# Agent attention with a squared-ReLU layer on one core: another order of the first blocks, and shared places for attention's matmuls

## Chip, cores and metric

One core of one Trainium2 chip. The metric is the device time of one execution in microseconds (us), median of the runs.

## What is computed

For each of B = 4 batches, `q`, `k` and `v` are 12480 x 128, with 49 agents; `w_in` is 128 x 2048, `w_out` 2048 x 128.

```
a2k     = softmax(agents @ k.T / sqrt(128))        # 49 x 12480
agent_v = a2k @ v                                  # 49 x 128
q2a     = softmax(q @ agents.T / sqrt(128))        # 12480 x 49
x       = q2a @ agent_v
y       = relu(x @ w_in) ** 2 @ w_out
```

## The kernel before

The queries are cut into 52 groups of 960 (13 of a batch). For a group and each of the 16 slices of 128 hidden columns there is one **block** i, from 0 to 831. Matmuls keep fp32 accuracy by splitting an operand into a rounded high part and the rest. `agent_v @ w_in` is made once a batch (`w_make`, parts `w_a` and `w_b`), so the first layer of a block (`mm1`, line 423) takes the 49 probabilities of each query (`p_a`, `p_b`) straight to the hidden slice: three pairs of matmuls. Two matmuls of a pair run on the two halves of TensorE's rows at once. ScalarE applies ReLU (`relu`, line 427) and squares (`square`, line 433) into `g`. `high` copies `g` to the rounded `gh`: by a DMA that GpSimd issues (line 438) for all blocks below 48 and for even ones after that, by VectorE else. `low` (VectorE, line 444) makes `gl = g - gh`. The second layer (`mm2`, line 462) is six pairs a block, from `gh` with `wo_hi` and `wo_lo` and from `gl` with `wo_hi`, added up over a group in one of two pairs of PSUM banks (`out`); from block 24 on two blocks are taken together. The first layer writes into two other pairs of banks (`h`, `new_h()`), by turns. Between two matmuls of `mm2` that change the bank of a row half stands a relay: an empty GpSimd instruction that waits for the first and frees the second.

Attention runs between the blocks. `q_scores` (line 169) makes the scores of two groups of queries, then six steps on VectorE and ScalarE turn them into probabilities (`q_turn`, `q_max`, `q_sub`, `q_exp`, `q_total`, `q_norm`, `q_back`), and eight DMAs of SyncE spread them (`q_spread`). For the next batch, keys come in seven parts (`k_scores`, then `k_copy` by ScalarE and `k_max` by VectorE), then `k_exp`, `k_turn`, and values in seven parts (`v_acc`, 28 matmuls on TensorE, then `v_sum` by VectorE). These matmuls use TensorE's rows as one, not as two halves. Before, `q_scores` and `v_acc` write into the pair of `out` banks that the current group doesn't use (`att()`, `bank()`), `k_scores` into `h`.

The order of everything is a list of (time, function), where time 1 is one block: `at(t, f, ...)`. Each engine works through its part of the sorted list in that order. The head up to block 24 is written by hand (lines 597 to 693 and 707 to 725); after that `chain()` looks for the first free time for a step, with `taken` and `banks` as the tables of what is in use. `SKIP` names blocks at which the second layer pauses. I call a **place** a point between two blocks at which attention's matmuls are inserted; `plan_queries`, `plan_keys` and `plan_values` choose them. In the head, `win_make` and `wo_make` convert the weights from 64-bit floats, four parts each, mostly on VectorE (`to_f32`, lines 85 to 90), and `wo_split` makes `wo_hi` by a DMA of GpSimd and `wo_lo` by a subtraction on GpSimd (two parts) or VectorE.

Of the kernel before, what the change touches and what calls it, by code (L numbers as in the profile page):

```python
# [13 lines left out]
AF = mybir.ActivationFunctionType  # L14
ALU = mybir.AluOpType
# [12 lines left out]
def agent_attention_relu2_kernel(ctx: ExitStack, tc: tile.TileContext, qT, kT, v, agT, w_in, w_out, outT):  # L28
# [6 lines left out]
    nc = tc.nc  # L35
# [5 lines left out]
    NSG = qT.shape[1] // ST  # L41
# [90 lines left out]
    kts, vts, pes, pss = {}, {}, {}, {}  # L132
# [4 lines left out]
    def new_h():  # L137
        return ps_h.tile([P, 2, 512], F32, name="h")
# [10 lines left out]
    def bank():  # L149
        return att()[:, 0]  # L150
# [74 lines left out]
    def v_acc(n, xs=(0, 1), ps=None):  # L225
        first, last = (n, n) if ps is None else (0, NP - 1)
        if ps is None:
            ps = pss["v", n] = bank()
        for x in xs:
            vt = vts.pop(2 * n + x)  # L230
            for y in range(VC):
                c = x * VC + y
                t = 64 * (c % 2)
                nc.tensor.matmul(ps[t:t + A, :C + 1], pes[n][:, c, :A], vt[:, y, :], start=n == first and c < 2, stop=n == last and c >= KC - 2)  # L234
            if x:
                pes.pop(n)
# [166 lines left out]
    hs, gs, ghs, gls = {}, {}, {}, {}  # L403
# [23 lines left out]
        nc.scalar.activation(gs[i], hs.pop(i)[:, :, :TT], AF.Relu)  # L427

    def square(i):
        if i in (1, 3):  # L430
            nc.gpsimd.tensor_tensor(gs[i], gs[i], gs[i], op=ALU.mult)
        else:
            nc.scalar.activation(gs[i], gs[i], AF.Square)  # L433

    def high(i):
        ghs[i] = ew.tile([P, 2, TT], F32R, name="gh", bufs=HB)
# [48 lines left out]

    LAG = 8
    TAIL = 36
    SKIP = (6, 9, 12)

    def by_dma(i):  # L490
        return i < NG - 4 and (i % 2 == 0 or i < 3 * NF)
# [3 lines left out]
    def at(t, f, *args):  # L495
        steps.append((t, len(steps), f, args))
# [5 lines left out]
    taken = {(e, s * NF + NF - 1 + LAG) for s in range(NSG) for e in ("DVE",)}  # L502
    banks = {s * NF + NF - 1 + LAG + x for s in range(NSG) for x in range(3)}
# [34 lines left out]

    def plan_queries(u):

        first, t = chain(max(18, 32 * u - 60), [("PE", q_scores, u), ("DVE", q_turn, u)])
        for x, s in enumerate(members(u)):
            at(first - LEAD + .1 * x, q_load, s)
        plan_rows(u, t + 2, 32 * u - 37)

    def plan_rows(u, g, free):
        todo = [("DVE", q_max, u), ("DVE", q_sub, u), ("ACT", q_exp, u), ("DVE", q_total, u), ("DVE", q_norm, u), ("DVE", q_back, u)]
        for e, f, _ in todo:
            _, t = chain(g, [(e, f, u)])
# [7 lines left out]
            _, t = chain(max(t, s * NF - 9 if s > 1 else 0), [("POOL" if s > 1 else "ACT", q_hi, s), ("DVE", q_lo, s)])  # L557
            assert t + 1 < s * NF, (s, t)

    def plan_keys(b, n, t):  # L560

        while ("PE", t) in keyed:
            t += 1
        keyed.add(("PE", t))
# [8 lines left out]
    keyed = set()  # L573
# [5 lines left out]
    def plan_values(b, t0, stop):  # L579

        used, turned = {}, {}
        d = (stop - TAIL - t0) / NP
        for n in range(NP):
            _, t1 = turned[n] = chain(max(t0 + 1 + int(n * d), used.get(n - 2, 0)), [("ACT", k_exp, n), ("DVE", k_turn, n)])
            used[n], end = chain(t1 + 3, [("PE", v_acc, n), ("DVE", v_sum, n)])
            for x in range(2):
                at(used[n] - LEAD + .1 * x, v_load, b, 2 * n + x)
        last, end = chain(end + 2, [("PE", a_final, 0), ("DVE", a_final, 1), ("DVE", a_final, 2)])
        assert end < stop - 6, (b, end, stop)
        if b < B - 1:  # L590
            for n in range(NP):
                _, keys = plan_keys(b + 1, n, used[n])
            return max(last + 2, plan_bias(keys + 1))


# [14 lines left out]
    Z = -100.0  # L610
    order, t = {}, 6.4
# [18 lines left out]
    for n, (f, *args) in enumerate(loads):  # L630
        t = order["v", 3] if f is q_load and args[0] else 0
# [15 lines left out]
    t = order["b", 3]  # L647
# [11 lines left out]
    t = order["q", 0] + 1.75  # L659
# [3 lines left out]
    t = last  # L663
# [7 lines left out]
    for n in range(2):  # L671
        for x, y in ((0, 2), (2, 3), (3, 3.5)):
            at(Z + t + y + .1 * n if n == 0 or x == 0 else .05 + .01 * x, w_first, x, n)
    for f, t in ((1, 1), (2, 2)):
        for x, y in ((0, .02), (2, .15), (3, .2)):
            at(t + y + (.1 if f == 2 and x else 0), w_make, 0, f, x)
    convert(win_make, 3, [y - Z for y in (6.7, 6.71, 6.72, 7.2, 7.7, 8.5)])
    for n, t, y0, y1 in ((0, (.13, .14, .15, .6, .7, .8), 2.35, 4.1), (1, (1.3, 1.31, 1.32, 2.1, 2.4, 2.45), 4.2, 6.2),
                         (2, (9.1, 9.11, 9.3, 10.1, 10.3, 11.1), 11.9, 14.3), (3, (12.1, 12.12, 12.3, 13.1, 13.3, 14.1), 14.9, 17.3)):
        convert(wo_make, n, [y - Z for y in t])  # L680
        at(y0, wo_split, n, 0)
        at(y1, wo_split, n, 1)
    for t in (1.45, 2.45, 4.45):
        at(t, warm_up, 3, 0)
    at(3.06, warm_up, 2, 0)
    at(3.07, begin)
    at(3.08, q_scores, 1)
    banks.update(range(12))
    for f, t in ((q_turn, 4), (q_max, 4.1), (q_sub, 4.6), (q_exp, 5.5), (q_total, 6.1), (q_norm, 6.6), (q_back, 7.6), (q_spread, 8.1)):
        at(t, f, 1)  # L690
    plan_halves(1, 13)
    for x, y in enumerate((.005, .02, .5, 1.4)):
        at(9 + y, w_make, 0, 3, x)
    for b in range(1, B):
        for f, x in enumerate((-6, -3, 0, 4)):
            first, end = chain(b * NS * NF + x, [("PE", w_make, b, f, 0), ("PX", w_make, b, f, 1), ("ACT", w_make, b, f, 2), ("DVE", w_make, b, f, 3)])
            assert x >= 4 * f - 12 and end < b * NS * NF + min(4 * f, LAG), (b, f, first, end)
    for u in range(2, NSG // 2 + 1):
        plan_queries(u)
    t = 20  # L700
    for n in range(NP):
        t, end = plan_keys(1, n, t + 3)
    ready = plan_bias(end + 1)
    for b in range(1, B):
        ready = plan_values(b, ready, b * NS * NF)

    for i in range(NG):
# [65 lines left out]
```

## Time and profile before

| | |
|---|---|
| median of 3 runs (lowest, highest) | 1740.31 us (1739.79, 1746.88) |
| the profiled execution's own time | 1742.1 us |
| its span, first to last instruction | 1740.3 us |
| mean granted TensorE clock | 0.997 |
| busy: PE / PEld | 99% / 86% |
| busy: VectorE / ScalarE / GpSimd | 86% / 92% / 16% |

The span is what the profile's rows cover; the profiled execution took 1.8 us more than it. A timeline row gives the start, the length, the engine, the line in the kernel, what is written from what, and the count; a bracket gives idle time before the row and what ended it. PE rows overlap, since matmuls are pipelined: starts are to be compared, not ends.

### The profile page before, as it was taken

Reading aid. Unit: us, or ns where it says so; the run is one execution under the profiler, and the core shown is the slowest. Engines: PE = TensorE matmul, PEld = TensorE weight load, DVE = VectorE, ACT = ScalarE, POOL = GpSimd, SP = SyncE. Lnnn points to the kernel's source line nnn. Section 1 sums busy time; section 2 is a strip of 40 time slices with the busy share of each in tenths; the row PEclk is TensorE's granted clock in tenths of the full one; section 3 lists DMA queues with packets and bytes.
Section 4 is the critical chain, followed back from the end, with each engine's and each line's share of the span. In section 5 each row is a group of like instructions: output and inputs, shape, how many; then the busy total and the mean of one; then the engine's idle time right before and its main releaser. Section 6 shows DMA issues by size and latency. Waiting matters only on the chain.

```text
span 1740.3 us, 41683 instructions
## 1 busy us (share of the span) xinstructions
PE 1717.3 (99%) x16833; PEld 1501.7 (86%) x16833; DVE 1490.3 (86%) x1744; ACT 1593.3 (92%) x1802; POOL 271.6 (16%) x508
## 2 busy tenths in 40 slices
PE   8899999999999999999999999999999999999998
PEld 4577888888888888988988898898898899999998
DVE  6877898898888898898898898898888889889887
ACT  4688998999998999999999999999999999999997
POOL 0322111111111111111111111111111111111110
PEclk9999999999999999999999999999999999999999
DMA  9799667648556646646646555565653555555452
GB/s 371 268 314 333 218 204 235 219 148 256 178 179 208 224 145 227 222 144 225 198 160 211 174 187 190 176 194 184 195 192 134 194 186 173 173 189 179 153 174 105
DMA packets 113506, 349.72 MB, mean 201 GB/s; under 512 B 15566, under 2 KB 28128, under 8 KB 113312
## 3 DMA queue, kind: packets, MB, share of 16 engines
q0 software_dynamic: 70976, 227.46, 38.6%
q1 hardware_dynamic: 42336, 119.59, 21.2%
q8 instruction: 132, 2.16, 0.5%
q14 instruction: 62, 0.51, 0.1%
HBM read 81.47 MB, written 25.56 MB: 61 GB/s over the span
## 4 chain that ended last, share of the span: by engine, by line
PE 91%; DMA 3%; issue 2%; DVE 2%; ACT 2%; SPq 0%; POOL 0%; DVEq 0%; POOLq 0%; ACTq 0%
PE out L462 55%; PE h L423 27%; PE ps_att L169 3%; PE ps_att L234 2%; PE h L169 2%; DMA gh<-g 2%; ACT g L433 1%; DMA vt<-v 1%; DVE gl L444 1%; PE ps_att L317 1%; DMA kt<-kT 1%; PE out L605 0%; PE out L234 0%; DVE e L353 0%; ACT g L427 0%
## 5 line engine op out<-in xcount | busy, mean ns | idle before, releaser
L444 DVE TENSOR_TENSOR gl<-g,gh 128x960 fp32r<-128x960 f32 x832 | 935.0, 1148 | 45.4 <-DMA gh<-g 37.2
L427 ACT ACTIVATE g<-h 128x960 f32<-128x960 f32 x832 | 812.8, 977 | 89.0 <-PE h L423 88.9
L433 ACT ACTIVATE g<-g 128x960 f32<-128x960 f32 x830 | 834.7, 1006 | 0.0
L462 PE MATMUL out<-gh,wo_hi 64*128 64x480 f32 x3328 | 621.7, 369 | 4.0 <-POOLq L456 3.3
L462 PE MATMUL out<-gh,wo_lo 64*128 64x480 f32 x3328 | 609.7, 362 | 0.0
L462 PE MATMUL out<-gl,wo_hi 64*128 64x480 f32 x3328 | 478.6, 364 | 3.5 <-DVE gl L444 3.5
L438 POOL DMA_DIRECT2D gh<-g x438 | 232.8, 531 | 1419.2 <-ACT g L433 727.3
L462 PEld LDWEIGHTS out<-gh,wo_hi 64*128 64x128 f32 x3328 | 314.2, 184 | 67.1 <-issue 36.3
L440 DVE CAST gh<-g 128x960 fp32r<-128x960 f32 x394 | 258.1, 655 | 127.0 <-ACT g L433 126.5
L462 PEld LDWEIGHTS out<-gl,wo_hi 64*128 64x128 f32 x3328 | 316.1, 186 | 28.6 <-DVE gl L444 7.9
L462 PEld LDWEIGHTS out<-gh,wo_lo 64*128 64x128 f32 x3328 | 317.4, 186 | 21.3
L423 PE MATMUL h<-p_a,w_a 49*128 49x480 f32 x1664 | 310.4, 369 | 0.6 <-ACT w_a L301 0.5
L423 PE MATMUL h<-p_a,w_b 49*128 49x480 f32 x1664 | 305.3, 363 | 0.0
L423 PE MATMUL h<-p_b,w_a 49*128 49x480 f32 x1664 | 304.4, 361 | 0.0
L423 PEld LDWEIGHTS h<-p_a,w_a 49*128 49x128 f32 x1664 | 158.8, 187 | 14.1 <-ACT w_a L301 1.5
L423 PEld LDWEIGHTS h<-p_b,w_a 49*128 49x128 f32 x1664 | 160.2, 188 | 10.3
L423 PEld LDWEIGHTS h<-p_a,w_b 49*128 49x128 f32 x1664 | 156.8, 184 | 12.6 <-DVE w_b L303 0.4
L353 DVE STREAM_TRANSPOSE e<-ps_att 128x960 f32<-128x960 f32 (+1 forms) x26 | 30.7, 1182 | 36.1 <-PE ps_att L169 36.1
L478 DVE COPY ob<-out 128x960 f32<-128x960 f32 x51 | 58.7, 1150 | 2.0 <-PE out L462 1.7
L184 ACT COPY sk<-h 128x896 f32<-128x896 f32 x28 | 25.3, 904 | 29.9 <-PE h L169 26.0
L169 PE MATMUL h<-kt,ag_sb 128*32 128x448 f32 x448 | 49.3, 545 | 1.9 <-DVE mxs L187 1.0
L169 PE MATMUL ps_att<-qt,ag_sb 128*32 128x480 f32 x408 | 47.2, 572 | 1.0 <-DVE w_b L328 1.0
(96 smaller groups left out, 585.0 us busy)
## 6 DMA issues: line engine op xcount, KB each, us to landing
gh<-g POOLq DMA_DIRECT2D x438, 480.0 KB, 3.5
vt<-v SPq DMA_DIRECT2D x56, 451.5 KB, 6.9
kt<-kT SPq DMA_DIRECT2D x56, 448.0 KB, 7.7
qt<-qT SPq DMA_DIRECT2D x52, 480.0 KB, 4.7
outT<-ob SPq DMA_DIRECT2D x51, 480.0 KB, 3.0
pt<-et SPq DMA_DIRECT2D x204, 60.0 KB, 3.6
p_a<-pt POOLq DMA_DIRECT2D x50, 211.9 KB, 3.5
raw<-w_in SPq DMA_DIRECT2D x4, 512.0 KB, 10.7
```

Source lines behind the costliest of these rows:

```text
L169: nc.tensor.matmul(ps[32 * j:32 * j + 32, h, :w], ags[j // 2][:, 32 * h:32 * h + 32], xs[j // 2][:, j % 2 * w:j % 2 * w + w], start=True, ...
L184: nc.scalar.copy(sk[:, n], pss["k", n][:, :, :KW])
L234: nc.tensor.matmul(ps[t:t + A, :C + 1], pes[n][:, c, :A], vt[:, y, :], start=n == first and c < 2, stop=n == last and c >= KC - 2)
L353: nc.vector.transpose(squares(es[u]), pss.pop(("q", u))[r, :, :TT].rearrange("p h (b c) -> p h b c", c=32))
L423: nc.tensor.matmul(hs[i][:, t, :TT], w, two(p), start=n == 0, stop=n == 2)
L427: nc.scalar.activation(gs[i], hs.pop(i)[:, :, :TT], AF.Relu)
L433: nc.scalar.activation(gs[i], gs[i], AF.Square)
L438: nc.gpsimd.dma_start(out=ghs[i], in_=gs[i])
L440: nc.vector.tensor_copy(ghs[i], gs[i])
L444: nc.vector.tensor_tensor(out=gls[i], in0=gs.pop(i), in1=ghs[i].bitcast(F32), op=ALU.subtract)
L462: mm = nc.tensor.matmul(o[:, u, :TT], w[rows, j, :], two(g[rows, u, :]), start=first and n == 0, stop=last and n == len(todo) - 1)
L478: nc.vector.tensor_copy(ob, o[:, :, :TT])
```

## The change

Five things are done.

1. Blocks 1 and 3 are squared by ScalarE like all others; before, GpSimd did it (`square`).
2. In the head, `w_make` of slices 1 and 2 stands at 0.5 and 1.6 (was 1 and 2), `w_make` of slice 3 at 7 (was 9), the conversion of the last part of `w_in` at 2 to 3 (was 6.7 to 8.5), that of `w_out`'s first two parts behind it; the second layer starts at block 6 (was 5) and pauses at 7 and 12 (was 6, 9 and 12); `low` of the first blocks comes 0.5 to 0.9 later, and blocks 6 to 9 take the timing of the later ones (`high` at i + 3.05, was i + 1.3).
3. `v_acc` writes into the first layer's banks (`new_h()`), with no gap kept for them in `banks`.
4. The planners share places: `shared` records the places of keys and values, `plan_queries` takes one of them where it finds one from 66 to 50 blocks before 32u, and the seven parts of batch 1's keys stand at 18 (two, with queries), 24 (two), 29 and 33 (two), where they had seven places of their own from 23 to 41.
5. Queries are planned after keys and values, and start up to two blocks earlier.

```
-            ps = pss["v", n] = bank()
+            ps = pss["v", n] = new_h()[:, 0]
...
-        if i in (1, 3):
-            nc.gpsimd.tensor_tensor(gs[i], gs[i], gs[i], op=ALU.mult)
-        else:
-            nc.scalar.activation(gs[i], gs[i], AF.Square)
+        nc.scalar.activation(gs[i], gs[i], AF.Square)
...
-    SKIP = (6, 9, 12)
+    SKIP = (7, 12)
...
-        first, t = chain(max(18, 32 * u - 60), [("PE", q_scores, u), ("DVE", q_turn, u)])
+        near = [t for t in sorted(shared) if 32 * u - 66 <= t <= 32 * u - 50 and t > rowed[-1] and not banks & set(range(t, t + 3))]
+        first, t = chain(near[0] if near else max(18, 32 * u - 62), [("PE", q_scores, u), ("DVE", q_turn, u)])
...
-            used[n], end = chain(t1 + 3, [("PE", v_acc, n), ("DVE", v_sum, n)])
+            t = t1 + 3
+            while t in shared or banks & set(range(t, t + 3)):
+                t += 1
+            used[n], end, shared[t] = t, t + 2, (b, n)
+            taken.add(("DVE", t))
+            at(t + .51, v_acc, n)
+            at(t + .55, v_sum, n)
...
-    for f, t in ((1, 1), (2, 2)):
-        for x, y in ((0, .02), (2, .15), (3, .2)):
-            at(t + y + (.1 if f == 2 and x else 0), w_make, 0, f, x)
-    convert(win_make, 3, [y - Z for y in (6.7, 6.71, 6.72, 7.2, 7.7, 8.5)])
+    for f, t in ((1, .5), (2, 1.6)):
+        for x, y in ((0, .005), (2, .02), (3, .56)):
+            at(t + y, w_make, 0, f, x)
+    convert(win_make, 3, [y - Z for y in (2, 2.01, 2.02, 2.6, 3, 3.02)])
...
-        at(9 + y, w_make, 0, 3, x)
+        at(7 + y, w_make, 0, 3, x)
...
-        t, end = plan_keys(1, n, t + 3)
+        t, end = plan_keys(1, n, (18, 18, 24, 24, 29, 33, 33)[n], "first")
...
-        if i < 10:
-            at(i + (1.3 if i else .2), high, i)
-            at(i + 4.4, low, i)
+        if i < 6:
+            at(i + (1.3 if i else .4), high, i)
+            at(i + (5.3 if i else 4.9), low, i)
```

The order shows three places. First VectorE in the head, from the first `low` on (`gl`). Before:

```order
L444 TENSOR_TENSOR gl<-g,gh 128x960
L361 TENSOR_TENSOR e<-e,mx 128x15x49
L444 TENSOR_TENSOR gl<-g,gh 128x960
L369 TENSOR_REDUCE sm<-e 128x15
L370 TENSOR_SCALAR sm<-sm 128x15
L371 RECIPROCAL sm<-sm 128x15
L444 TENSOR_TENSOR gl<-g,gh 128x960
L375 TENSOR_TENSOR e<-e,sm 128x15x49
L85 TENSOR_SCALAR cv_p<-raw 128x512
L87 TENSOR_SCALAR cv_x<-raw 128x512
L88 SCALAR_TENSOR_TENSOR cv_x<-raw,cv_x 128x512
```

And in the change, from the same point:

```order
L441 TENSOR_TENSOR gl<-g,gh 128x960
L357 TENSOR_REDUCE mx<-e 128x15
L361 TENSOR_TENSOR e<-e,mx 128x15x49
L441 TENSOR_TENSOR gl<-g,gh 128x960 x2
L369 TENSOR_REDUCE sm<-e 128x15
L370 TENSOR_SCALAR sm<-sm 128x15
L371 RECIPROCAL sm<-sm 128x15
L375 TENSOR_TENSOR e<-e,sm 128x15x49
L441 TENSOR_TENSOR gl<-g,gh 128x960
L328 SCALAR_TENSOR_TENSOR w_b_696<-ps_att,rc,w_a_695 113x512
```

The conversion of `w_in`'s last part (`cv_p`, `cv_x` from `raw`) no longer stands between the first `low`s, `q_max` (`mx`, line 357) has moved behind the first `low`, and the `w_b` of slice 3 follows the fourth `low`.

Second, TensorE after the first layer of block 18 (a row counts instructions, of which a score or value matmul makes two in the trace). Before:

```order
L423 MATMUL h<-p_a,w_b_498 128x480 x2
L462 MATMUL out<-gh,wo_hi 128x480 x2
L462 MATMUL out<-gh,wo_lo 128x480 x2
L462 MATMUL out<-gl,wo_hi 128x480 x2
L169 MATMUL ps_att<-qt,ag_sb 32x480 x8
L462 MATMUL out<-gh,wo_hi 128x480 x2
```

And now:

```order
L423 MATMUL h<-p_a,w_b_498 128x480 x2
L459 MATMUL out<-gh,wo_hi 128x480 x2
L459 MATMUL out<-gh,wo_lo 128x480 x2
L459 MATMUL out<-gl,wo_hi 128x480 x2
L169 MATMUL ps_att<-qt,ag_sb 32x480 x8
L169 MATMUL h<-kt,ag_sb 32x448 x16
L459 MATMUL out<-gh,wo_hi 128x480 x2
L459 MATMUL out<-gh,wo_lo 128x480 x2
```

Two parts of keys follow the queries, where each had a place of its own.

Third, TensorE where values come after queries: before, block 100, with values and keys seven blocks later,

```order
L423 MATMUL h<-p_b,w_a_535 128x480 x2
L423 MATMUL h<-p_a,w_b_536 128x480 x2
L169 MATMUL ps_att<-qt,ag_sb 32x480 x8
L462 MATMUL out<-gh,wo_hi 128x480 x2
L462 MATMUL out<-gh,wo_lo 128x480 x2
```

and in the change block 106:

```order
L423 MATMUL h<-p_a,w_b_696 128x480 x2
L169 MATMUL ps_att<-qt,ag_sb 32x480 x8
L234 MATMUL h<-vt,pe 49x129 x14
L169 MATMUL h<-kt,ag_sb 32x448 x8
L459 MATMUL out<-gh,wo_hi 128x480 x2
L459 MATMUL out<-gh,wo_lo 128x480 x2
```

Queries, values and keys stand in a row, and the values go to `h`. From block 18 on there were 53 places for queries, keys and values (25 of queries, 7 of keys, 21 of values, 14 of these with keys); in the change there are 41.

## Rows read from the trace of the kernel before

**Rows 1.** Page, part 1: busy time, share of the span, instructions of each engine
```profile
PE 1717.3 (99%) x16833; PEld 1501.7 (86%) x16833; DVE 1490.3 (86%) x1744; ACT 1593.3 (92%) x1802; POOL 271.6 (16%) x508
```

**Rows 2.** Stretches: busy us (count) of PE, PEld, DVE, ACT, POOL; clock, DMA share, GB/s
```profile
75.00:100.00 25.00, 20.88 (x180) 16.57 (x180) 18.71 (x26) 20.66 (x24) 5.83 (x11) 0.93 0.85 272
125.00:150.00 25.00, 25.00 (x238) 17.45 (x236) 18.13 (x18) 20.08 (x23) 5.51 (x11) 1.00 1.13 344
200.00:300.00 100.00, 100.00 (x1008) 85.75 (x1006) 85.64 (x99) 90.76 (x105) 13.84 (x26) 1.00 0.67 225
```

**Rows 3.** Timeline of PE: start, us, line, out<-in, count; a place for queries
```profile
346.70 0.36 PE L423 MATMUL h<-p_a,w_b 49*128 49x480 f32 x2
347.00 1.82 PE L169 MATMUL ps_att<-qt,ag_sb 128*32 128x480 f32 x16
348.75 0.47 PE L462 MATMUL out<-gh,wo_hi 64*128 64x480 f32 x2
349.05 0.36 PE L462 MATMUL out<-gh,wo_lo 64*128 64x480 f32 x2
```

**Rows 4.** Timeline of PE: values and keys in one place
```profile
367.21 1.75 PE L234 MATMUL ps_att<-vt,pe 128*49 128x129 f32 x28
368.89 1.71 PE L169 MATMUL h<-kt,ag_sb 128*32 128x448 f32 x16
```

**Rows 5.** Timeline of DVE, 60 to 91 us
```profile
60.74 0.92 DVE L357 TENSOR_REDUCE mx<-e 128x15 f32<-128x735 f32 x1
61.58 3.27 DVE L444 TENSOR_TENSOR gl<-g,gh 128x960 fp32r<-128x960 f32 x1
...
70.31 0.42 DVE L85 TENSOR_SCALAR cv_p<-raw 128x512 uint32<-128x512 uint32 x1
...
73.87 0.65 DVE L89 SCALAR_TENSOR_TENSOR cv_p<-raw,cv_p 128x512 uint32<-128x512 uint32 x1
...
75.51 0.68 DVE L90 SCALAR_TENSOR_TENSOR win_sb<-cv_x,cv_p 128x512 f32<-128x512 f32 x1
...
87.86 1.16 DVE L444 TENSOR_TENSOR gl<-g,gh 128x960 fp32r<-128x960 f32 x1 [2.38 <-DMA gh<-g]
...
90.14 0.65 DVE L400 TENSOR_TENSOR p_b<-pt,p_a 113x480 fp32r<-113x480 f32 x1
```

**Rows 6.** Timeline of POOL, its tensor operations of the head
```profile
62.02 1.80 POOL L431 TENSOR_TENSOR g<-g 128x960 f32<-128x960 f32 x1
...
66.95 1.28 POOL L113 TENSOR_TENSOR wo_lo<-wo_f,wo_hi 128x512 fp32r<-128x512 f32 x1
```

**Rows 7.** Timeline of PE, end of the head, with the idle time before a row
```profile
89.97 0.47 PE L462 MATMUL out<-gh,wo_hi 64*128 64x480 f32 x2 [2.16 <-POOLq L456]
...
91.59 0.61 PE L423 MATMUL h<-p_b,w_a 49*128 49x480 f32 x2
...
94.79 0.37 PE L423 MATMUL h<-p_a,w_a 49*128 49x480 f32 x2
...
96.62 0.37 PE L423 MATMUL h<-p_a,w_a 49*128 49x480 f32 x2
```

**Rows 8.** DMA issues from 76 to 92 us: count, size, median us to landing
```profile
gh<-g POOLq DMA_DIRECT2D x5, 480.0 KB, 4.8
```

**Rows 9.** Timeline of PE, values of one place and the next first-layer block
```profile
226.45 1.71 PE L169 MATMUL h<-kt,ag_sb 128*32 128x448 f32 x16
...
229.41 0.37 PE L423 MATMUL h<-p_a,w_a 49*128 49x480 f32 x2
```

**Rows 10.** Timeline of VectorE, the sum of the same values
```profile
228.89 0.59 DVE L244 TENSOR_TENSOR acc<-ps_att,acc 49x129 f32<-49x129 f32 x2
```

**Rows 11.** Page, part 6: issues of keys, count, size, median us to landing
```profile
kt<-kT SPq DMA_DIRECT2D x56, 448.0 KB, 7.7
```

**Rows 12.** Timeline of PE around the longest wait for a copy after the head
```profile
609.46 0.47 PE L462 MATMUL out<-gh,wo_hi 64*128 64x480 f32 x2 [0.25 <-DMA gh<-g]
...
610.72 0.67 PE L462 MATMUL out<-gl,wo_hi 64*128 64x480 f32 x4 [0.19 <-DVE gl L444]
```

More of the change, by code (lines that the diff above doesn't have):

```diff
@@ L539, in plan_queries @@
     def plan_queries(u):
-        first, t = chain(max(18, 32 * u - 60), [("PE", q_scores, u), ("DVE", q_turn, u)])
+        near = [t for t in sorted(shared) if 32 * u - 66 <= t <= 32 * u - 50 and t > rowed[-1] and not banks & set(range(t, t + 3))]
+        first, t = chain(near[0] if near else max(18, 32 * u - 62), [("PE", q_scores, u), ("DVE", q_turn, u)])
+        print('Q', u, first, t, first in shared, 32 * u - 16)
         for x, s in enumerate(members(u)):
@@ L544, in plan_queries @@
         plan_rows(u, t + 2, 32 * u - 37)
+    rowed = [0]
     def plan_rows(u, g, free):
@@ L550, in plan_rows @@
             g = t + (3 if u > 2 else 2)
+        print('rows', u, t)
+        back = t
         t = max(t, free)
+        rowed.append(back)
         at(t + .9, q_spread, u)
@@ L558, in plan_halves, with plan_keys @@
             assert t + 1 < s * NF, (s, t)
-    def plan_keys(b, n, t):
-        while ("PE", t) in keyed:
+    def plan_keys(b, n, t, key=None):
+        while t in shared and shared[t] != key:
             t += 1
-        keyed.add(("PE", t))
+        shared[t] = key
         at(t + .52, k_scores, b, n)
@@ L571, in plan_keys @@
         return t, end
-    keyed = set()
+    shared = {}
     def plan_bias(t):
@@ L591, in plan_values @@
             for n in range(NP):
-                _, keys = plan_keys(b + 1, n, used[n])
+                _, keys = plan_keys(b + 1, n, used[n], (b, n))
             return max(last + 2, plan_bias(keys + 1))
@@ L673, in agent_attention_relu2_kernel @@
             at(Z + t + y + .1 * n if n == 0 or x == 0 else .05 + .01 * x, w_first, x, n)
-    for f, t in ((1, 1), (2, 2)):
-        for x, y in ((0, .02), (2, .15), (3, .2)):
-            at(t + y + (.1 if f == 2 and x else 0), w_make, 0, f, x)
-    convert(win_make, 3, [y - Z for y in (6.7, 6.71, 6.72, 7.2, 7.7, 8.5)])
-    for n, t, y0, y1 in ((0, (.13, .14, .15, .6, .7, .8), 2.35, 4.1), (1, (1.3, 1.31, 1.32, 2.1, 2.4, 2.45), 4.2, 6.2),
+    for f, t in ((1, .5), (2, 1.6)):
+        for x, y in ((0, .005), (2, .02), (3, .56)):
+            at(t + y, w_make, 0, f, x)
+    convert(win_make, 3, [y - Z for y in (2, 2.01, 2.02, 2.6, 3, 3.02)])
+    for n, t, y0, y1 in ((0, (.6, .61, .62, 1.15, 1.2, 1.3), 2.3, 4.1), (1, (3.2, 3.21, 3.3, 3.6, 3.7, 3.8), 5, 7),
                          (2, (9.1, 9.11, 9.3, 10.1, 10.3, 11.1), 11.9, 14.3), (3, (12.1, 12.12, 12.3, 13.1, 13.3, 14.1), 14.9, 17.3)):
@@ L682, in agent_attention_relu2_kernel @@
         at(y1, wo_split, n, 1)
-    for t in (1.45, 2.45, 4.45):
+    for t in (1.45, 2.45, 4.45, 5.45):
         at(t, warm_up, 3, 0)
@@ L687, in agent_attention_relu2_kernel @@
     at(3.08, q_scores, 1)
-    banks.update(range(12))
-    for f, t in ((q_turn, 4), (q_max, 4.1), (q_sub, 4.6), (q_exp, 5.5), (q_total, 6.1), (q_norm, 6.6), (q_back, 7.6), (q_spread, 8.1)):
+    banks.update(range(11))
+    for f, t in ((q_turn, 4.04), (q_max, 5.5), (q_sub, 5.51), (q_exp, 6.5), (q_total, 7.5), (q_norm, 7.51), (q_back, 8.5), (q_spread, 8.9)):
         at(t, f, 1)
@@ L697, in agent_attention_relu2_kernel @@
             assert x >= 4 * f - 12 and end < b * NS * NF + min(4 * f, LAG), (b, f, first, end)
-    for u in range(2, NSG // 2 + 1):
-        plan_queries(u)
-    t = 20
     for n in range(NP):
-        t, end = plan_keys(1, n, t + 3)
+        t, end = plan_keys(1, n, (18, 18, 24, 24, 29, 33, 33)[n], "first")
     ready = plan_bias(end + 1)
@@ L705, in agent_attention_relu2_kernel @@
         ready = plan_values(b, ready, b * NS * NF)
+    for u in range(2, NSG // 2 + 1):
+        plan_queries(u)
     for i in range(NG):
@@ L710, in agent_attention_relu2_kernel @@
         at(i + .1, relu, i)
-        at(i + (1.2 if i else .105), square, i)
-        if i < 10:
-            at(i + (1.3 if i else .2), high, i)
-            at(i + 4.4, low, i)
+        at(i + (1.2 if i else .3), square, i)
+        if i < 6:
+            at(i + (1.3 if i else .4), high, i)
+            at(i + (5.3 if i else 4.9), low, i)
         elif by_dma(i):
```

## Prediction

> **What bounds the kernel now.** I read the page's busy times first, then stretches of the span, then TensorE's timeline in a quiet stretch and in the head, then the engines that it waits for there. PE is busy 99% [rows 1], which says little by itself, so the stretches decide: from 200 to 300 us PE is busy for all of the 100 us, while VectorE, ScalarE and the DMAs have room; from 75 to 100 us it is busy for 20.88 of 25 us, at a mean granted clock of 0.93 [rows 2]. So there are two kinds of time to win: what PE itself spends between blocks after the head, and what it waits for in the head.
>
> After the head. Two matmul pairs of one block start 0.20 us apart. At a place for queries the last pair of the first layer starts at 346.70, the scores at 347.00, the second layer at 348.75, its next pair at 349.05 [rows 3]. Both 0.30 us steps are 0.10 longer than 0.20: going from half rows to whole rows costs 0.10, and going back another 0.10. The scores between take 1.75 us and have to be done anyway. Where values and keys share a place, 28 value matmuls start at 367.21 and the keys at 368.89 [rows 4]: 1.68 us, 0.06 each, with nothing extra between the two kinds.
>
> The head. The first `low` of VectorE starts at 61.58 and takes 3.27 us [rows 5], where a later one takes 1.16 [rows 5]; in that time GpSimd squares block 3, 62.02 to 63.82 [rows 6]. From there VectorE works without a break until it waits 2.38 us for a copy; that `low` (block 8) ends near 88.93 and the rest of a conversion follows. PE stands still for 2.16 us before 89.97 [rows 7]: the relay that it waits for is behind a copy of `wo_hi` in GpSimd's queue, which needs that conversion. Then the granted clock falls to the lower of its two levels: pairs start 0.40 us apart from 91.59 until 94.79 [rows 7], where PE had been idle shortly before. So **VectorE's chain from the first `low` to block 8's `low` sets the end of the head**, and block 18 begins at 96.62 [rows 7].
>
> **The change, part by part.**
>
> *Start of VectorE's chain.* The matmul of `w_make` for slice 1 now follows block 0 directly, so that slice 2's `w_b` is ready some 2.2 us earlier by my walk through the order; but the conversion of `w_in`'s last part is now ahead of the first `low`, and `q_max` behind it, which takes the 2.2 us back. I put the start of the first `low` where it was, 61.6; ends: 1 us to either side.
>
> *GpSimd's squares.* The first `low` takes 1.16 instead of 3.27: 2.1 us less. ScalarE gets two squares of some 0.9 us; it is covered by ScalarE's waits for PE in the head, and would cost 1.8 us without them.
>
> *Moved conversion.* Five operations leave the stretch between the first and the ninth `low`. Three have rows, 0.42, 0.65 and 0.68 [rows 5], and the other two are of the first and the second kind: 2.8 us of durations, 2.6 us from start to start. `q_max` comes in, 60.74 to 61.58 [rows 5], 0.84. Net 1.8 us less.
>
> *The wait for block 8's copy*, 2.38 us [rows 5]. The copy is now issued about 1.75 blocks later in the order, but its `low` is also later in the order. Copies around it take 4.8 us from issue to landing [rows 8]; I count 6 us from its issue to its turn on VectorE, so the wait goes: 2.4 us less. Ends: 0 (it stays) to 2.4.
>
> *GpSimd's second subtraction for `wo_lo`*, 1.28 us [rows 6], now falls near the third `low`, as the square did near the first: between 0 and 1.3 us, I take 0.65, the middle, since nothing in the rows puts it on one side.
> A rule speaks to this: the Trainium skill, page "SBUF — State Buffer", section "SBUF: two separate sides", says that VectorE and GpSimd share a pair of ports by an exclusive lock that whoever starts first holds for a whole instruction. By it the square's 2.1 us is explained, though the row shows VectorE's operation starting first and yet the longer one; and the subtraction would cost its whole 1.3 us whenever the two meet, and the sum would be 5.8 us less instead of 6.4.
>
> *`p_b` of group 1*, 0.65 us [rows 5], stands in front of block 9's `low` before, behind it now, and block 16 waits for it: 0.6 us more.
>
> The relay's wait and the fall of the clock stay, since the `wo_hi` copy still stands ahead of that relay in GpSimd's queue. Three more warm-up matmuls on PE lie where it waits for the first `low`: nothing. Sum of the head: 2.1 + 1.8 + 2.4 - 0.65 - 0.6 = 5.0 us less.
>
> *Shared places.* From block 18 on 53 places become 41, and each of the 12 gone saves 0.10 + 0.10 us: 2.4 us less. The bound below is 1.6, were a step inside a shared place as dear as half a switch at the eight places where values follow queries.
> On this too there is a rule: the Trainium skill, page "TensorEngine Tiling (Array Packing)", section "Key Properties", says that a change of tiling mode drains TensorE. Queries, values and keys have different column widths, so by the rule a shared place would still pay inside; the trace shows 1.68 us for 28 value matmuls and no step before the keys [rows 4], so I stay with 2.4; by the rule the sum would be 5.6 us less instead of 6.4.
>
> *Values in the first layer's banks.* A first-layer block can only begin when `v_sum` has read its bank. In a late case the values ended at 226.45, the next block began at 229.41 [rows 9], and the sum started at 228.89 and took 0.59 [rows 10]: done 0.07 us too late. The sum now stands right behind the values in VectorE's order, which is earlier than here. At 21 places that is between 0 and 1.5 us, I take 0. The other side: `out`'s spare banks are free of values, and that is what lets queries share.
>
> *Later places and their loads.* Keys of batch 1 that had 18 blocks now have 15, while copies to `gh` still go by DMA for every block. Their transfers after block 18 are ten loads of 448 KB [rows 11], 15 copies of 480 KB [rows 8], and some 1.2 MB of the rest (a store, probabilities of two groups): 13.2 MB in 32.7 us (15 blocks of 1.83 and two later places of 3.4 and 1.8 us), or 404 GB/s. The trace shows 344 GB/s with the DMAs fully shared out [rows 2]. The pipeline can be some 4 us late before PE stops, so I take 1 us more; ends 0 and 5.7 us (13.2 MB at 344 GB/s is 38.4 us). Each of the seven later places of three kinds has six loads at once; the longest wait for a copy after the head cost PE 0.25 + 0.19 us [rows 12], and I leave that at no change, since loads already came in such heaps.
>
> **Sum.** 5.0 + 2.4 - 1.0 = 6.4 us less. The profiled execution takes 1742.1 (span 1740.3 and 1.8 around it), so 1735.7 for it; it stands 1.8 above the median of 1740.31. I forecast the median: **1733.9 us**. A measurement here can tell about 0.5%, 8.7 us, from no change: faster means below 1731.6, slower above 1749.0.
>
> **Rivals.**
>
> *A head without a throttle.* If VectorE meets neither the subtraction nor `p_b` (0.65 + 0.6), the loads cost nothing (1.0), and the relay's wait is too short for the clock to fall (8 pairs from 91.59 to 94.79 took 3.2 us, where 0.20 each gives 1.6: 1.6 us), 3.85 us more are gained: 1730.1. For it: each of the three is near its edge by my walk. Against: I count the relay's wait at 1.3 to 2 us, not far from the 2.16 that came before the fall.
>
> *The head stays.* The copies of blocks 6 to 9 are issued 1.75 blocks, 3.2 us, later. If they take over 6 us as block 8's did, VectorE waits as long as before: of the 5.0 us the 2.4 go and up to 2.1 of the rest with them. Left are 0.5 + 2.4 - 1.0 = 1.9 us: 1738.4. For it: block 8's `low` has already waited once. Against: the loads for queries that ran into that copy now come after it.
>
> *DMA-bound, slower than before.* The DMAs give 344 GB/s and no more, so the keys cost 5.7 us, the late copies eat the head's gain as above (0.5 left), and each of some 14 places whose loads come in a heap costs PE the 0.44 us of [rows 12], 6.2 us: 5.7 + 6.2 - 0.5 - 2.4 = 9.0 us slower, 1749.3. It decides if copies wait over 4 us for the loads. Against: in the stretch at 344 GB/s PE was busy for all of its 25 us [rows 2].
>
> **Chances.** The forecast 0.52, with 1731 to 1737 as its own range; the head without a throttle 0.25; the head that stays 0.16; DMA-bound 0.07. The last ends on the edge of slower, with half of its cases between 1740 and 1749. Faster by over 0.5%: the second case and the lower end of the first, 0.36; slower 0.05; within 0.5%, 0.59. The range that should hold the time 8 times in 10 reaches from 1728 (all favourable ends, with the first `low` a us earlier as well) to 1740 (the head that stays with part of the DMA's price).
>
> **What would show it.** Right: the first `low` at about 1.2 us long; no idle time before block 8's `low`; block 18 beginning near 91.6, 5 us earlier than 96.62; PE busy for all of each stretch after 110 us, and 0.30 us steps only at 41 places. Wrong in the head: block 18 near 96, with waits of VectorE for copies between 75 and 90. Wrong after it: PE idle between 95 and 130 us with the releaser a copy or a load of keys, or first-layer blocks that wait for the sum of values. If block 18 begins 5 us earlier and the end doesn't follow, the loss is between the two, and the stretch that has it names its cause.

## The result and the profile after

The changed kernel takes 1756.03 us (median of 4 runs, 1754.29 to 1756.43) against 1740.05 for the kernel before beside it (4 runs): **16.0 us slower**, ratio 1.0081 with a 95% interval of 1.0055 to 1.0106. The forecast was 1733.9 with a range from 1728 to 1740, so the sign was wrong too. Its profiled execution spans 1754.1 us, 13.8 more than before. The medians from here on are of executions in the fast state; of the kernel with values in `h` alone one execution, of 7403.29 us against 1744.19 to 1749.40 for the other four, is left out as slow.

The busy times (page, part 1) show PE 5.8 us busier than in [rows 1]; its idle time grew as well.

```profile
PE 1723.1 (98%) x16836; PEld 1498.6 (85%) x16836; DVE 1491.5 (85%) x1744; ACT 1594.6 (91%) x1804; POOL 268.2 (15%) x506
```

The stretches of the changed kernel, with the columns of [rows 2]:

```profile
75.00:100.00 25.00, 21.10 (x180) 14.56 (x180) 20.15 (x24) 19.30 (x24) 5.79 (x10) 0.93 0.87 283
100.00:125.00 25.00, 23.25 (x224) 18.38 (x223) 15.24 (x17) 19.82 (x23) 5.86 (x11) 1.00 1.08 350
125.00:150.00 25.00, 25.00 (x246) 19.65 (x244) 19.63 (x23) 22.88 (x26) 6.04 (x12) 1.00 0.79 268
150.00:175.00 25.00, 22.53 (x200) 17.90 (x198) 14.66 (x17) 18.77 (x22) 6.14 (x12) 0.93 1.02 343
200.00:300.00 100.00, 99.08 (x990) 83.54 (x988) 84.91 (x101) 90.36 (x104) 13.85 (x27) 1.00 0.68 226
```

The gap in the first row is the head's and was there before. From 100 to 125 PE now stands idle for 1.8 us and from 150 to 175 for 2.5 (0 and 0.4 before), the latter with a clock of 0.93, both with the DMAs fully shared out; and from 200 to 300 us PE is no longer busy throughout. I went from there to PE's timeline and looked for each step longer than 0.20 us a pair.

**The head.** VectorE, GpSimd and PE in the head of the changed kernel, from three timelines:

```profile
58.95 2.04 DVE L89 SCALAR_TENSOR_TENSOR cv_p<-sk,cv_p 128x512 uint32<-128x512 uint32 x1 [0.55 <-ACT cv_p L86]
...
62.73 1.12 DVE L441 TENSOR_TENSOR gl<-g,gh 128x960 fp32r<-128x960 f32 x1
...
65.55 2.41 DVE L441 TENSOR_TENSOR gl<-g,gh 128x960 fp32r<-128x960 f32 x1
...
86.63 1.16 DVE L441 TENSOR_TENSOR gl<-g,gh 128x960 fp32r<-128x960 f32 x1 [1.57 <-DMA gh<-g]
```
```profile
59.15 1.29 POOL L113 TENSOR_TENSOR wo_lo<-wo_f,wo_hi 128x512 fp32r<-128x512 f32 x1
...
65.66 1.28 POOL L113 TENSOR_TENSOR wo_lo<-wo_f,wo_hi 128x512 fp32r<-128x512 f32 x1
```
```profile
84.80 0.47 PE L459 MATMUL out<-gh,wo_hi 64*128 64x480 f32 x2 [1.06 <-POOLq L453]
...
88.41 0.47 PE L423 MATMUL h<-p_b,w_a 49*128 49x480 f32 x2 [1.92 <-DVE p_b L400]
...
93.64 0.37 PE L423 MATMUL h<-p_a,w_a 49*128 49x480 f32 x2
```

The first `low` is short, as forecast, but it starts 1.15 later than in [rows 5]: ahead of it a conversion takes 2.04, where the same step takes 0.68 later on (at 76.41), since it meets GpSimd's first subtraction. The second `low` meets the second subtraction and takes 1.26 longer than the usual 1.15. VectorE still waits 1.57 for the copy that it waited 2.38 for. PE's wait for the relay has halved against [rows 7], and a new one stands behind it, 1.92 us for `p_b`. Block 18 begins at 93.64, 3.0 earlier than in [rows 7], not 5.0.

**Copies late.** PE in the stretches with the first keys and just after them, then the DMA issues from 150 to 175 us (count, size, median us to landing), and after these the copies of the kernel before in the same stretch:

```profile
109.77 0.47 PE L459 MATMUL out<-gh,wo_hi 64*128 64x480 f32 x2 [0.66 <-DMA gh<-g]
111.14 0.47 PE L459 MATMUL out<-gh,wo_hi 64*128 64x480 f32 x2 [0.69 <-DMA gh<-g]
...
164.21 0.77 PE L459 MATMUL out<-gh,wo_hi 64*128 64x480 f32 x2 [1.68 <-DMA gh<-g]
164.77 0.60 PE L459 MATMUL out<-gh,wo_lo 64*128 64x480 f32 x2
...
166.03 0.61 PE L423 MATMUL h<-p_a,w_a 49*128 49x480 f32 x2
166.43 0.61 PE L423 MATMUL h<-p_b,w_a 49*128 49x480 f32 x2
```
```profile
gh<-g POOLq DMA_DIRECT2D x11, 480.0 KB, 10.2
qt<-qT SPq DMA_DIRECT2D x2, 480.0 KB, 8.1
vt<-v SPq DMA_DIRECT2D x2, 451.5 KB, 11.3
kt<-kT SPq DMA_DIRECT2D x2, 448.0 KB, 12.7
```
```profile
gh<-g POOLq DMA_DIRECT2D x11, 480.0 KB, 5.3
```

A copy that took 5.3 us before (4.8 in [rows 8]) takes 10.2, and after the wait of 1.68 the pairs stand 0.40 apart: the lower of the clock's two levels.

**Values late.** PE and ScalarE at one of the later places:

```profile
1038.16 0.37 PE L423 MATMUL h<-p_a,w_b 49*128 49x480 f32 x2
1039.06 1.75 PE L234 MATMUL h<-vt,pe 128*49 128x129 f32 x28 [0.53 <-ACT g L427]
```
```profile
1033.40 1.24 ACT L211 ACTIVATE sk<-sk,mb 128x448 f32<-128x448 f32 x2
...
1038.01 1.00 ACT L427 ACTIVATE g<-h 128x960 f32<-128x960 f32 x1
```

The values start 0.90 behind the last pair, where 0.30 is normal [rows 3]. They need the first layer's bank that this ReLU reads; ScalarE is late since it has done a `k_exp` three blocks before. Five places show this wait, with 0.60 to 0.75 more than the 0.30.

**Loads late.** PE at a place with queries, values and keys:

```profile
692.73 1.00 PE L169 MATMUL ps_att<-qt,ag_sb 128*32 128x480 f32 x4
694.75 1.80 PE L169 MATMUL ps_att<-qt,ag_sb 128*32 128x480 f32 x12 [1.02 <-DMA qt<-qT]
696.49 1.75 PE L234 MATMUL h<-vt,pe 128*49 128x129 f32 x28
```

The second load of queries isn't there when the first is used up.

### The profile page after: what moved, and what is told of

Same layout as the page of the kernel before. It is cut to its first block, busy times and chain, and to the rows that moved or that the text cites. A ratio compares the mean times of both kernels' runs of the same rounds, so it can differ in the third digit from the quotient of the medians.

```text
span 1754.1 us, 41710 instructions
## 1 busy us (share of the span) xinstructions
PE 1723.1 (98%) x16836; PEld 1498.6 (85%) x16836; DVE 1491.5 (85%) x1744; ACT 1594.6 (91%) x1804; POOL 268.2 (15%) x506
## 3 DMA queue, kind: packets, MB, share of 16 engines
q8 instruction: 132, 2.16, 0.5%
## 4 chain that ended last, share of the span: by engine, by line
PE 70%; ACT 10%; DMA 8%; issue 6%; DVE 5%; SPq 0%; DVEq 0%; POOLq 0%; ACTq 0%
PE out L459 42%; PE h L423 21%; ACT g L430 6%; DMA gh<-g 5%; ACT g L427 3%; DVE gl L441 3%; PE ps_att L169 3%; PE h L234 2%; PE h L169 2%; DMA qt<-qT 2%; DMA vt<-v 1%; ACT sk L211 1%; PE ps_att L317 1%; DVE gh L437 1%; DMA kt<-kT 0%
```

## The experiments

Four theories, one for each part of the change, came from these lines. **A:** the denser first keys make copies late through the DMAs, and the waits lower the clock. **B:** values in the first layer's banks wait for ReLU. **C:** the six loads of a shared place, issued at one point, make each other and the copies late. **D:** in the head `low`, then `p_b`, sets the end. The rival of each is that its waits come from another part. All ratios are to runs of the kernel before on the same chip; "us" are differences of medians on one chip, and where two changed kernels are compared, it is by that column. Chips differ too: the medians of the kernel before go from 1739.49 to 1740.74.

| kernel | median us | ratio (95%) | us |
|---|---|---|---|
| changed | 1756.03 | 1.0081 (1.0055, 1.0106) | +16.0 |
| head alone | 1738.61 | 0.9988 (0.9979, 0.9997) | -2.1 |
| head, dense first keys | 1749.16 | 1.0048 (1.0031, 1.0064) | +8.4 |
| these and values in `h` | 1751.70 | 1.0067 (1.0054, 1.0081) | +12.2 |
| values in `h` alone | 1746.68 | 1.0039 (1.0024, 1.0054) | +5.9 |
| changed, places half a block later | 1749.37 | 1.0051 (1.0036, 1.0066) | +8.6 |
| changed, loads spread | 1749.71 | 1.0056 (1.0040, 1.0071) | +9.0 |
| changed, first keys as before | 1746.99 | 1.0035 (1.0025, 1.0045) | +6.3 |
| changed, 12 copies by VectorE | 1749.16 | 1.0056 (1.0039, 1.0072) | +9.7 |
| squares alone | 1737.69 | 0.9989 (0.9980, 0.9998) | -1.8 |
| head, `p_b` ahead | 1736.53 | 0.9978 (0.9968, 0.9987) | -4.2 |
| that, loads spread | 1736.76 | 0.9981 (0.9972, 0.9990) | -3.9 |
| changed, all four mended | 1737.32 | 0.9988 (0.9980, 0.9997) | -2.2 |

The ratios' intervals of two changed kernels often overlap. What carries the comparisons with the changed kernel is that all its executions took 1754.29 us or more, and none of the other kernels' counted executions more than 1754.06. Where the executions of two kernels overlap, the text says so.

**The head alone**: the kernel before with items 1 and 2, of which this is a part:

```
-    SKIP = (6, 9, 12)
+    SKIP = (7, 12)
...
-        at(9 + y, w_make, 0, 3, x)
+        at(7 + y, w_make, 0, 3, x)
```

> Only items 1 and 2 of the change, the head; places, banks and first keys as before. In the changed kernel block 18 began 3.0 us earlier than before (5.0 had been forecast). Theory A, the head's gain is lasting and the loss is all behind it: 3 us less than before, 1737. Rival, the blocks behind the head give the 3 us back by themselves, since copies and VectorE are late there: 1740, with waits for copies between 95 and 170 us.

2.1 us less, between the two expectations, and from 100 to 150 us PE is busy throughout. So the gain of the head lasts, and the loss lies behind it. PE waits longer for `p_b` here than in the changed kernel (2.60), and yet the clock stays up (stretch with PE alone: busy, count, clock, DMA share, GB/s):

```profile
75.00:100.00 25.00, 20.79 (x190) 1.00 0.91 296
```

**Squares alone**: the kernel before with item 1.

```
-        if i in (1, 3):
-            nc.gpsimd.tensor_tensor(gs[i], gs[i], gs[i], op=ALU.mult)
-        else:
-            nc.scalar.activation(gs[i], gs[i], AF.Square)
+        nc.scalar.activation(gs[i], gs[i], AF.Square)
```

> The kernel before with item 1 alone: ScalarE squares blocks 1 and 3. Theory D, the long first low delays VectorE's whole chain to the end of the head: 2.1 us less than before, 1738.6, block 18 near 94.5. Rival, block 8's copy is what the chain waits for anyway, so VectorE only waits longer there: no change, 1740.7, block 18 near 96.6.

1.8 us less. As theory D had it, the long `low` was on the path. But this one line gives about as much as the whole head: item 2 adds nothing that shows beside it. In this run's profile block 18 begins at 92.43, earlier than the 94.5 expected: VectorE doesn't wait for the copy of [rows 5] at all (it waits 1.37 for ScalarE there), and PE has no wait like the 2.16 of [rows 7].

**The head with `p_b` ahead.** In the head alone VectorE stood idle for a copy ahead of block 9's `low`, with `p_b` behind that:

```
-    plan_halves(1, 13)
+    at(13.5, q_hi, 1)
+    at(14.25, q_lo, 1)
+    taken.update({("ACT", 13), ("DVE", 14)})
+    chain(2 * NF - 9, [("POOL", q_hi, 2), ("DVE", q_lo, 2)])
```

> The head alone, and in it p_b of group 1 on VectorE ahead of the wo_lo subtraction and of block 9's low, where VectorE had stood idle 1.6 us for a copy. Theory D, the new wait of TensorE for p_b (2.6 us in the head alone, 1.9 in the changed kernel) is all that kept block 18 from coming earlier: 1.5 to 2.6 us less than the head alone, 1736 to 1737, block 18 near 91.5. Rival, block 8's and 9's copies and their lows are as late and take its place: 1738 to 1739.

2.1 us less than the head alone by medians; the intervals of the two ratios overlap a little. VectorE's timeline: `p_b` is done before the wait, which stays and now costs PE only 0.52.

```profile
83.93 0.66 DVE L400 TENSOR_TENSOR p_b<-pt,p_a 113x480 fp32r<-113x480 f32 x1
84.50 0.69 DVE L113 TENSOR_TENSOR wo_lo<-wo_f,wo_hi 128x512 fp32r<-128x512 f32 x1
87.26 1.16 DVE L441 TENSOR_TENSOR gl<-g,gh 128x960 fp32r<-128x960 f32 x1 [2.07 <-DMA gh<-g]
```

This is the lowest median here, below both the kernel before and the changed one: without the shared places, and with values where they were.

**That, with loads spread:**

```
-                at(t - LEAD + .1 * x, k_load, b, 2 * n + x)
+                at(t - 6.5 - 1.1 * (1 - x) if b > 1 else t - LEAD + .1 * x, k_load, b, 2 * n + x)
...
-                at(used[n] - LEAD + .1 * x, v_load, b, 2 * n + x)
+                at(used[n] - 8.7 - 1.1 * (1 - x), v_load, b, 2 * n + x)
```

> The one before, and loads spread: from batch 2's keys on, values 9.8 and 8.7 blocks ahead of use, keys 7.6 and 6.5, queries 7 as before. Theory C, the copies that were late at 669, 734 and 799 us in the head alone (1.1 to 1.2 us of TensorE each) meet a heap of loads: 2 to 4 us less than the one before, 1733 to 1735. Rival, those copies collide with something else, or others do then: no change, 1736 to 1737.

No change, as the rival had it: the heaps of two or four loads that these places have cost nothing that shows.

**Head and dense first keys**: the head alone, and

```
-    t = 20
-        t, end = plan_keys(1, n, t + 3)
+        t, end = plan_keys(1, n, (18, 18, 24, 24, 29, 33, 33)[n], "first")
```

> The head and the first keys at 18, 18, 24, 24, 29, 33, 33; queries and values planned as before, values in the spare banks of out. Theory A, the denser keys cost TensorE what the changed kernel shows between 105 and 170 us, waits for copies of 0.8, 0.9, 0.6 and 1.9 us and 2.2 us at the lower clock, 6 us, against some 0.8 for four places less: 1742, 5 more than with the head alone. Rival, those waits come from values and queries elsewhere in the plan: 1736 to 1737, no waits over 0.4 us there.

10.5 us more than the head alone, twice theory A's 5, with values and queries as they were. Its PE timeline and a stretch of 5 us show why the price was too low:

```profile
110.27 0.47 PE L459 MATMUL out<-gh,wo_hi 64*128 64x480 f32 x2 [0.52 <-DMA gh<-g]
...
112.04 0.47 PE L459 MATMUL out<-gh,wo_hi 64*128 64x480 f32 x2 [1.10 <-DMA gh<-g]
113.23 0.77 PE L459 MATMUL out<-gl,wo_hi 64*128 64x480 f32 x2 [0.32 <-DVE gl L441]
...
115.13 5.43 PE L169 MATMUL h<-kt,ag_sb 128*32 128x448 f32 x32
```
```profile
115.00:120.00 5.00, 5.00 (x30) 1.33 (x32) 5.00 (x6) 3.49 (x4) 1.07 (x2) 0.54 1.11 348
```

In the changed kernel's profile the same two parts come behind much the same waits (0.66, 0.69 and 0.39), at the full clock:

```profile
113.41 3.21 PE L169 MATMUL h<-kt,ag_sb 128*32 128x448 f32 x32
```

They take 3.21 us there and 5.43 here, at a clock of 0.54, behind 1.94 us of waits. The profiled execution took 1754.06, the longest of this kernel's four, so it shows more of the loss than the median has.

**The changed kernel with the first keys at 23 to 41 again:**

```
+    t = 20
-        t, end = plan_keys(1, n, (18, 18, 24, 24, 29, 33, 33)[n], "first")
+        t, end = plan_keys(1, n, t + 3)
```

> The changed kernel with the first keys at 23, 26, ... 41 again, one part at a place; all else as changed. Theory A (dense keys make copies late, then the clock falls): the waits between 105 and 175 us go, 5 to 9 us less than the changed kernel, 1747 to 1751. Rival, with this kernel's other places the same waits turn up elsewhere: 1755 to 1757.

9.7 us less than the changed kernel, the most that any one part gives back; PE's idle time between 105 and 150 us is gone and that from 150 to 175 falls to 0.44. So A holds in the full change too.

**The changed kernel with fewer copies by DMA**, in the same stretch:

```
-        return i < NG - 4 and (i % 2 == 0 or i < 3 * NF)
+        return i < NG - 4 and (i % 2 == 0 or i < 24)
```

> The changed kernel with the copies of the 12 odd blocks from 25 to 47 made by VectorE instead of by DMA, in the stretch of the first keys: 5.9 MB less on the DMAs there. Theory A, copies are late there because key loads and copies share the DMAs: the waits between 105 and 175 us shrink to under 1 us, 4 to 7 us less than the changed kernel, 1749 to 1752. Rival, VectorE or ScalarE lags behind the double places: VectorE has 0.65 us more for each of the 12 blocks and the waits stay or grow, 1756 to 1760.

6.3 us less, against the rival, though VectorE has more to do. From 150 to 175 us PE is busy throughout again; the waits from 109 to 112 stay, since their copies are of blocks too early to be taken off:

```profile
100.00:125.00 25.00, 23.39 (x208) 17.21 (x206) 13.12 (x15) 18.10 (x21) 5.34 (x10) 0.93 1.07 357
150.00:175.00 25.00, 25.00 (x248) 20.97 (x246) 21.58 (x26) 23.23 (x27) 3.97 (x8) 1.00 0.76 261
```

**Values in the first layer's banks alone**, in the kernel before:

```
-            ps = pss["v", n] = bank()
+            ps = pss["v", n] = new_h()[:, 0]
```

> The kernel before with one line changed: values are summed in the first layer's banks; every place, load and head as before. Theory B, values wait there for the ReLU of the block before last and what is behind them for the sum: 0.3 to 0.4 us at each of 21 places, 6 to 8 us more than before, 1746 to 1748, with waits of the value matmuls for ReLU in most places. Rival, the values of the changed kernel are late through loads that come in heaps of six, not through the banks: 1740, no such waits.

5.9 us more. Five of 21 places show the wait for ReLU, not most of them, 3.5 us in all (waits of PE: total, times, longest); summed from the last pair to the first value matmul the 21 places lose 4.6, and copies that are later than before account for 2 more in this profile. Those need not come from the values: the head alone has its values where they were, and its profile loses 2.9 us against that of before between block 60 and the end.

```profile
PE h L234 <- ACT g L427: 3.5, 5, 0.8
```

**The changed kernel with its places behind the second layer of the next block**, in `at()`:

```
+        if t >= 18 and f in (q_scores, q_turn, v_acc, k_scores, v_sum, k_copy):
+            t += .505 - .0099 * (t % 1 - .5) * 100 + .01 * (t % 1 - .5)
```

> The changed kernel with all of attention's matmuls (queries, values, keys) half a block later, behind the second-layer pairs of the next block and ahead of its first-layer pairs, so that ReLU has six more pairs, 1.2 us, to free the bank. Theory B, values wait for ReLU: those waits (3.9 us at places without queries, part of 3.7 at places with them) go, 4 to 7 us less than the changed kernel, 1749 to 1752. Rival, loads and copies are what is late: 1755 to 1757.

7.4 us less, and PE has no idle time ahead of values for ReLU any more (their weight loads wait 0.9 us for it in all). So B's mechanism holds, but the 7.4 aren't all B's. Of the 6.6 us between the two profiles 4.3 arise behind block 60, where 4 to 7 were expected in all; the rest lies ahead of it, and PE's idle time from 105 to 125 us is smaller too, first the changed kernel, then this one (columns of [rows 2]):

```profile
105.00:125.00 20.00, 18.25 (x176) 13.74 (x174) 13.10 (x14) 15.28 (x18) 4.71 (x9) 1.00 1.11 361
105.00:125.00 20.00, 19.61 (x194) 14.38 (x190) 14.19 (x16) 16.94 (x20) 5.34 (x10) 1.00 1.11 376
```

**Queries in places of their own**: the head, the dense first keys, and values by the line just shown; the planners of queries and values are those of before:

```
-        near = [t for t in sorted(shared) if ...]
-        first, t = chain(near[0] if near else max(18, 32 * u - 62), ...)
+        first, t = chain(max(18, 32 * u - 60), ...)
```

> The head, the dense first keys and the values in the first layer's banks, but queries planned as before, in places of their own: what is missing of the change is the sharing of queries alone. Theory C, a shared place saves 0.2 us but its heap of six loads costs some 1.6 us at three places of batch 2: 8 places, 1.6 dearer, 4.8 cheaper, 3 us less than the changed kernel, 1753. Rival, sharing brings its saving and no cost: 1757 to 1758.

3.8 us less than the changed kernel: sharing the queries, with six loads at one point, costs more than it saves. Against the head with the dense first keys this kernel has the values in `h` and nothing else, and there the executions overlap: that 3.8 isn't clear of noise by itself, as values alone are.

**The changed kernel with loads spread** over five blocks:

```
-            at(first - LEAD + .1 * x, q_load, s)
+            at(first - 8.7 - 1.1 * (1 - x) if u > 2 else first - LEAD + .1 * x, q_load, s)
...
-                at(t - LEAD + .1 * x, k_load, b, 2 * n + x)
+                at(t - 6.5 - 1.1 * (1 - x) if b > 1 else t - LEAD + .1 * x, k_load, b, 2 * n + x)
...
-                at(used[n] - LEAD + .1 * x, v_load, b, 2 * n + x)
+                at(used[n] - 10.9 - 1.1 * (1 - x), v_load, b, 2 * n + x)
```

> The changed kernel with the loads of a place no longer issued all at one point: from batch 2's keys on, values 12.0 and 10.9 blocks ahead of their use, queries 9.8 and 8.7, keys 7.6 and 6.5 (were 7 for all). Theory C, after 350 us some 5 us are lost because six loads in a heap make copies, queries and values late: those waits go (queries split by 0.7 and 1.0 us, 2.3 between queries and values, copies of 0.3 to 0.9), 4 to 6 us less than the changed kernel, 1750 to 1752. Rival, the banks alone cost the time there: 1755 to 1757.

7.0 us less. Of the difference of the profiles, 4.8 us arise between the queries at 569 and at 812 us, where the three heaps of batch 2 are; 0.9 is gained ahead of that. A shared place there now runs without a gap:

```profile
754.49 1.82 PE L169 MATMUL ps_att<-qt,ag_sb 128*32 128x480 f32 x16
756.24 1.75 PE L234 MATMUL h<-vt,pe 128*49 128x129 f32 x28
757.92 1.71 PE L169 MATMUL h<-kt,ag_sb 128*32 128x448 f32 x16
```

From queries to values are 1.75 us, as from queries to the second layer in [rows 3]. Where keys follow queries in the changed kernel, it is 1.64:

```profile
94.95 1.82 PE L169 MATMUL ps_att<-qt,ag_sb 128*32 128x480 f32 x16
96.59 3.19 PE L169 MATMUL h<-kt,ag_sb 128*32 128x448 f32 x32
```

Queries and keys write the same form (32 columns), values another (49). So a step of some 0.11 stays in the shared place where the form changes, and one of the same size stands behind queries in a place of their own.

**All four mended at once**: `p_b` ahead, first keys as before, loads spread, and values in `h` only within two blocks of queries (`asked` holds those places).

```
-            ps = pss["v", n] = new_h()[:, 0]
+            ps = pss["v", n] = new_h()[:, 0] if place in asked else bank()
```

> The changed kernel with each loss taken out: p_b ahead in the head, first keys at 23 to 41, loads spread, and values in the first layer's banks only where queries stand just ahead of them or close by, else in the spare banks of out. If theories A to D are the whole of it, the shared places are left as a gain of some 2 us on top of the better head: 1733 to 1735, below the head with p_b alone (1736.5). Rival, places with three kinds cost more than they save whatever their loads and banks: 1737 to 1742.

18.2 us less than the changed kernel, and as far below before as the head alone: A to D cover all of the loss. But it isn't below the head with `p_b` ahead (1736.5; the intervals overlap), and 1737.3 lies in the range of the rival, not in the 1733 to 1735 expected: the shared places leave no gain that can be seen, and where the 2 us that they were to leave went isn't shown.

## Why the prediction was wrong

The steps add up: head -2.1, dense keys +10.5, values +3.8, shared queries +3.8, together +16.0. Each is known to about 3 us, and they aren't independent: values alone cost 5.9.

1. *Bound.* Right: PE outside the head had no slack, and so every new wait of it would go into the time.
2. *Head, 5.0 less.* **Sized wrongly**: 2.1 by medians. The square's term (2.1) was right, 1.8 measured. Four others were not. The start of the first `low`, left where it was with 1 us to either side, is 1.15 later, by a conversion that met GpSimd's first subtraction. The second subtraction cost 1.26, all of its 1.28, not the middle, 0.65. The rule quoted from the Trainium skill, page "SBUF — State Buffer", section "SBUF: two separate sides", has this price, and its 1.3 should have been taken; who was first can't be read from the rows, since VectorE's begins 0.11 ahead of GpSimd's. The wait for a copy, 2.4 less, is 0.8 less (1.57 is left). And `p_b` was read wrongly: the `low` that waits is VectorE's tenth and so block 9's, not block 8's, and `p_b` follows it in [rows 5] as it does now (at 87.70). Before, PE's wait for the relay, which hung on the same `low`, hid that; now it shows as 1.92. Besides, the wait of 2.38 was in part this one execution's. In two runs with the old order of the head, squares alone and values alone, VectorE doesn't wait for that copy (it waits 1.37 and 2.00 for ScalarE), PE has no wait like the 2.16 of [rows 7], and in values alone, whose head is that of before, block 18 begins 1.8 earlier. The prediction said that the profiled execution stood 1.8 above the median and took the whole gain off the median all the same.
3. *Shared places, 2.4 less.* The size was about right, its parts were not. By the starts of blocks in PE's timeline, a block takes 1.83, with queries 3.77, with keys 3.66, with two parts of keys 5.17, with values and keys 5.34, with all three kinds 7.09 where nothing is late. So queries cost 1.94 by themselves and 1.75 ahead of values and keys, 0.19 saved at eight places; the second part of keys in a place costs 1.51 instead of 1.83, 0.32 saved at three, and queries ahead of two parts of keys (6.78) save as much at one more: 2.8 in all. The rule of the Trainium skill, page "TensorEngine Tiling (Array Packing)", section "Key Properties", agrees with this: 0.13 less is saved where the form changes. That holds between values and keys too (values alone 3.70: 0.19 saved together), so the 1.68 of [rows 4] wasn't free of a step, as the prediction read it.
4. *Values in `h`, 0, ends 0 and 1.5.* **Failed.** Of the ring of two banks I costed only the side behind the values (the next block waits for `v_sum`), not the side ahead: the bank that values take is the one that ReLU of the block before last must free, and they ask for it 1.2 us, six pairs, sooner than the next block would. ScalarE, 91% busy, is just then behind by a `k_exp`.
5. *First keys, 1.0 more, ends 0 and 5.7.* **Failed**, by the largest amount. The sum (404 GB/s wanted, 344 to be had) was right, and 350 are seen. But I let 4 us of lateness go unpaid and charged the rest at its own length. The copies took 7 to 10 us, PE stood, and where the clock fell to the lower level, pairs took twice as long (0.40 us); in the changed kernel's profile that is in the second stretch, 150 to 175. Also missed: the values and queries of batch 1 come earlier too, so their six loads meet the last stretch in which every block copies by DMA (162 us).
6. *Six loads at once, no change.* **Failed**: 7.0 by the run with loads spread; by the profiles 4.8 arise where the three heaps of batch 2 are. It had been excused with the small waits that loads in heaps of four caused before.

The rival that came nearest was the one on the other side, DMA-bound, at 0.07: its mechanism was right, its number, 1749.3, still 6.7 too low, since it left out the banks and the clock. It spread the price of the loads over some 14 places of 0.44 us; most of it came at three. What would show the prediction wrong was named rightly: PE idle between 95 and 130 us with a copy as the releaser.

The price of the clock in step 5 can be read from three kept profiles with the same matmuls from block 20 to block 35, behind much the same idle time. From 105 to 125 us (columns of [rows 2]), first queries in places of their own, then the head with dense first keys (the changed kernel's row stands above, with 18.25):

```profile
105.00:125.00 20.00, 18.30 (x174) 12.47 (x170) 15.30 (x17) 15.94 (x19) 4.81 (x9) 1.00 1.12 375
105.00:125.00 20.00, 18.06 (x142) 11.56 (x140) 14.07 (x16) 12.81 (x15) 3.97 (x8) 0.83 1.10 365
```

At a clock of 1.00 the 15 blocks take 39.0 us (39.1 in the changed kernel), at 0.83 they take 42.4. So the lower clock costs 3.3 us there, more than the 1.9 of idle time. Why it falls in one execution and not in another isn't shown.

## What to carry to other kernels

Where a buffer is lent to another user, cost both edges: who must free it for the guest, and when, as well as who waits behind the guest; read it against the engine that frees it at its latest, not at its average. Where a stretch already asks for what the DMAs give, price added transfers by the latency of the copies that share them, not by the mean rate, and add what the clock takes after the stall. A wait seen in one execution of the head should be looked for in a second one before its removal is counted.

## What the hardware showed

The fall of the clock after a stall isn't the same each time: with idle times of 1.06 and 1.92 us in the head the changed kernel's granted clock was 0.93 from 75 to 100 us, with 1.02 and 2.60 the head alone kept 1.00. Behind waits of 1.7 to 1.9 us the same two parts of keys took 3.21 or 5.43 us.

VectorE's `low` that began 0.11 us ahead of GpSimd's subtraction still took 1.26 longer and ended 1.02 after it; the `low` of [rows 5] ended 1.03 after the square. In both cases VectorE's operation ends as if it had begun only when GpSimd's was done.

Attention's matmuls between half-row pairs cost 0.32 us a place beyond themselves, and 0.13 for each change of form within a place (block lengths above). And the same head differed by 1.8 us between two executions.
